# Loading half of a weight matrix ahead of the input and moving the tables behind it, at the start of a fused FFT-attention and feed-forward kernel

## The chip, the cores and the metric

The kernel runs on one core of a Trainium2 chip. The metric is the device time of one execution in microseconds (us); where several runs are given it is their median, with the range in brackets. The span of a profile is the time from its first to its last instruction and lies some 1.8 to 1.95 us below the device time of the same run. In the profiles PE is the matrix engine (TensorE) and PEld its loading of weights, DVE is VectorE, ACT is ScalarE, POOL is GpSimd, and SP is SyncE, which here issues DMAs. A profile is one execution.

## The reference, cut to what matters

```python
X  = rfft(x, axis=1)                        # x: 8 batches x 3008 x 256, f32
Yr = Xr @ w_r - Xi @ w_i + b_r              # w_r, w_i: 256 x 256
Yi = Xr @ w_i + Xi @ w_r + b_i
Yr, Yi = soft_threshold(Yr, 0.01), soft_threshold(Yi, 0.01)
y  = irfft(Yr + 1j * Yi, n=3008)            # viewed as 24064 rows of 256
r  = maximum(y @ w_in, 0)                   # w_in: 256 x 2048
out = (s * r * r + b) @ w_out               # w_out: 2048 x 256
```

## The kernel before: what the change and the argument touch

The Fourier transform over 3008 = 94 x 32 is done with matrices: `A_t` (94 points), `F_t` and `F_2` (32 points, forward), `T_t` (inverse). The first batch goes through alone, then the feed-forward part of one batch runs beside the transforms of the next. The first batch's x comes in eight half chunks on GpSimd's DMA queue, which casts f32 to f16. Everything else comes on SyncE's queue.

```python
A_t = cpool.tile(...); nc.sync.dma_start(out=A_t[0:N1, :], in_=A_d)
emit_load_x(0)                              # 8 half chunks, GpSimd's queue
for w in (w_r, w_i):                        # whole W, SyncE's queue: beside x
    st = rpool.tile([P, DC, D], F32, name="w_st", tag="rt")
    nc.sync.dma_start(out=st, in_=w.rearrange("(c p) e -> p c e", p=P))
    w_st.append(st)
...
def emit_load_inverse():                    # the whole tables
    nc.sync.dma_start(out=T_t[:, 0:H], in_=t_d[:, 0:H])
    nc.sync.dma_start(out=F_t[:, H:], in_=f_d)
    nc.sync.dma_start(out=F_2[1], in_=f_2_d)
    t_load = nc.sync.dma_start(out=T_t[:, H:], in_=t_d[:, H:])
    ...                                     # small things
def emit_load_weights():                    # w_in (2 loads), then w_out (4), GpSimd's queue
    ...
def place_w():                              # f32 staging -> f16 W_t, on ACT
    for i in range(2):
        nc.scalar.copy(out=W_t[:, :, i], in_=w_st[i])
def sum_w_out():                            # GpSimd: 7 adds, column sums of w_out for the bias b
    ...
# in the first batch, after each half chunk g (c, h = divmod(g, 2)):
if c == 2: emit_load_inverse(); place_f(slice(0, 4))     # only after its second half
if c == 1: place_w()
...
gate = nc.gpsimd.tensor_copy(out=w_in_t[0][0:1, 0:1], in_=F_t[0:1, H, 0:1])
with tc.issue_after(gate.ins):              # "the gate": waits until the rest of F_t is there
    emit_load_x(1)                          # second batch
    emit_load_weights()
...
# feed-forward, per 2 x 512 results: ACT takes the relu out of PSUM, DVE squares it
nc.scalar.activation(out=rt[:, :, 0:w], in_=ps[:, :, 0:w], func=AF.Relu)
nc.vector.tensor_tensor(out=gt[:, :, 0:w], in0=rt[:, :, 0:w], in1=rt[:, :, 0:w], op=ALU.mult)
```

The transform of a later batch writes `u` (three buffers), stores it to DRAM as `ud` and loads it back turned as `us`.

## Time and profile before

| | before |
|---|---|
| device time | 846.94 us (846.37 to 847.2, 3 runs) |
| span of the profile | 844.6 us |
| last half chunk of x reaches PE | 13.77 us |
| first matmul with W ("mixing starts") | 14.68 us |
| gate opens | 17.43 us |
| first output evacuated | 62.35 us |

The page's first rows give, for each engine, busy time, its share of the span and the number of instructions:

```profile
PE 835.1 (99%) x6654; PEld 601.3 (71%) x6654; DVE 694.7 (82%) x1034; ACT 640.6 (76%) x862; POOL 45.9 (5%) x73
```

Read this as: PE sets the time. Whatever the change wins or loses must show as PE starting its steady work sooner or later, or as PE idling, or else after PE's last matmul. Two moments are therefore followed: the start of mixing, and the first output. What lies between (47.67 us in this profile, 62.35 - 14.68) is called the middle; after the first output PE runs nearly without a gap.

### The profile page before, as it was taken

The numbers are of one execution on the slowest core, as the hardware profiler recorded it, in microseconds if no ns is written. First come the engines' busy times: TensorE is split into PE (matmuls) and PEld (weight loads), VectorE is DVE, ScalarE is ACT, GpSimd is POOL, SyncE is SP. The second block draws the span as 40 slices with busy tenths as digits, with TensorE's granted clock in tenths as the row PEclk, the third lists the DMA queues.
The fourth block names the chain that finished last, engine by engine and source line by source line (L and its number), as shares of the span: only waits on it lengthen the run. The fifth ranks groups of instructions, "written<-read, shape, count | busy, mean of one in ns | idle before, by whom it ended". The sixth has DMA issues, their size and how long they took to land.

```text
span 844.6 us, 17119 instructions
## 1 busy us (share of the span) xinstructions
PE 835.1 (99%) x6654; PEld 601.3 (71%) x6654; DVE 694.7 (82%) x1034; ACT 640.6 (76%) x862; POOL 45.9 (5%) x73
## 2 busy tenths in 40 slices
PE   8999999999999999999999999999999999999998
PEld 7857767777677766777677776777667777766765
DVE  5999987888888988888888888798978888776674
ACT  5987887778778877788777787778877778666673
POOL 4630000000000001000000000000000000000000
PEclk9999999999999999999999999999999999999999
DMA  7955467224851367324761247613354223411111
GB/s 200 181 151 118 119 161 199 74 77 98 202 156 54 103 171 188 93 70 107 189 174 50 81 101 196 172 43 90 106 152 125 59 78 97 113 33 38 38 44 50
DMA packets 105939, 96.06 MB, mean 114 GB/s; under 512 B 9607, under 2 KB 97675, under 8 KB 104515
## 3 DMA queue, kind: packets, MB, share of 16 engines
q1 hardware_dynamic: 99362, 80.55, 32.9%
q0 software_dynamic: 6496, 14.42, 10.6%
q8 instruction: 52, 0.85, 0.4%
q14 instruction: 29, 0.23, 0.1%
HBM read 53.52 MB, written 46.66 MB: 119 GB/s over the span
## 4 chain that ended last, share of the span: by engine, by line
PE 92%; ACT 3%; DVE 2%; DMA 1%; issue 1%; POOL 0%; DVEq 0%; ACTq 0%; POOLq 0%
PE psa L852 38%; PE psh L781 37%; PE psf L647 4%; PE psf L582 3%; PE psf L633 2%; PE psf L677 2%; PE psf L618 2%; PE psf L730 2%; ACT rt L788 1%; DMA x<-in_x_dram 1%; PE psm L425 1%; POOL x L213 0%; ACT yt L170 0%; DVE z L463 0%; PE psf L456 0%
## 5 line engine op out<-in xcount | busy, mean ns | idle before, releaser
L788 ACT ACTIVATE rt<-psh 128x1024 f32<-128x1024 f32 (+2 forms) x384 | 387.2, 1009 | 120.2 <-PE psh L781 118.8
L795 DVE TENSOR_TENSOR gt<-rt 128x1024 f16<-128x1024 f32 (+2 forms) x319 | 382.3, 1202 | 94.4 <-ACT rt L788 93.4
L852 PE MATMUL psa<-w_out_t,gt 128*128 128x256 f16 (+1 forms) x3024 | 454.4, 272 | 0.1
L852 PEld LDWEIGHTS <-gt 128*128 128x128 f16 (+1 forms) x3024 | 300.9, 101 | 186.6 <-issue 1.1
L781 PE MATMUL psh<-yt,w_in 128*128 128x512 f16 (+1 forms) x1344 | 396.8, 378 | 0.2 <-ACT rt L788 0.2
L781 PEld LDWEIGHTS <-w_in 128*128 128x128 f16 x1536 | 142.7, 98 | 26.2 <-issue 1.2
L862 DVE SCALAR_TENSOR_TENSOR ost<-psa,s_bc,bias_bc 128x512 f32<-128x512 f32 (+2 forms) x97 | 71.1, 733 | 9.6 <-PE psa L852 7.9
L792 ACT ACTIVATE gt<-rt 128x1024 f16<-128x1024 f32 (+2 forms) x65 | 68.2, 1050 | 0.9
L652 DVE TENSOR_TENSOR ring<-psf,s 128x512 f16<-128x512 f32 x84 | 57.6, 685 | 3.3 <-PE psf L647 3.2
L170 ACT CAST v<-psf 128x512 f16<-128x512 f32 x77 | 44.8, 582 | 19.4 <-PE psf L677 19.4
L170 ACT CAST xf<-psf 128x512 f16<-128x512 f32 x79 | 46.3, 586 | 8.8 <-PE psf L618 8.8
L781 PE MATMUL psh<-tail,w_in 128*128 128x512 f16 (+1 forms) x192 | 52.1, 353 | 0.0
L170 ACT CAST u<-psf 96x512 f16<-96x512 f32 x74 | 42.8, 580 | 11.2 <-PE psf L582 10.9
L647 PE MATMUL psf<-W_g,xf 128*128 128x256 f16 x336 | 50.4, 273 | 0.0
L170 ACT CAST yt<-psf 128x480 f16<-128x480 f32 (+2 forms) x76 | 39.0, 520 | 14.7 <-PE psf L730 14.2
L213 POOL DMA_DIRECT2D x<-in_x_dram x36 | 18.8, 527 | 432.9 <-PE psf L582 431.7
L582 PE MATMUL psf<-x,A_t 94*96 94x512 f16 x102 | 38.9, 382 | 1.0 <-ACT yt L170 0.6
L658 DVE TENSOR_TENSOR ring<-ring,high 128x512 f16<-128x512 f16 x84 | 35.6, 423 | 2.3
L659 DVE TENSOR_TENSOR ring<-ring 128x512 f16<-128x512 f16 x84 | 35.6, 423 | 2.1
L657 DVE TENSOR_TENSOR ring<-ring,low 128x512 f16<-128x512 f16 x84 | 35.5, 422 | 1.6
L647 PEld LDWEIGHTS <-xf 128*128 128x128 f16 x336 | 32.9, 98 | 4.1 <-issue 0.2
L730 PE MATMUL psf<-C_t,vs 96*128 96x96 f16 x448 | 33.2, 205 | 0.0
(100 smaller groups left out, 508.6 us busy)
## 6 DMA issues: line engine op xcount, KB each, us to landing
out_dram<-ost SPq DMA_DIRECT2D x152, 128.0 KB
ud<-u SPq DMA_DIRECT2D x28, 384.0 KB
us<-ud SPq DMA_DIRECT2D x28, 384.0 KB
vd<-v SPq DMA_DIRECT2D x42, 256.0 KB
vs<-vd SPq DMA_DIRECT2D x14, 768.0 KB
x<-in_x_dram POOLq DMA_DIRECT2D x28, 376.0 KB, 6.3
ring<-ring SPq DMA_DIRECT2D x280, 32.0 KB
out_dram<-ost SPq DMA_DIRECT2D x16, 120.0 KB
```

The costliest lines, as they stand in the source:

```text
L170: return None, nc.scalar.copy(out=dst, in_=src)
L582: nc.tensor.matmul(ps[0:96, :], A_t[0:N1, :], x16[(b, c)][0:N1, j * D : (j + 2) * D], start=True, stop=True,)
L647: nc.tensor.matmul(ps[:, r, :], xt[:, 2 - r, dc], W_g[:, dc, r], start=(dc == 0), stop=(dc == DC - 1),)
L652: nc.vector.tensor_tensor(out=t, in0=ps, in1=hold[i // 2][:, i % 2].unsqueeze(1).to_broadcast([P, 2, D]), op=ALU.add,)
L658: nc.vector.tensor_tensor(out=m, in0=m, in1=high, op=ALU.min)
L730: nc.tensor.matmul(ps[:, j * 96 : (j + 1) * 96], vs[(b, h)][:, k, ec * P : (ec + 1) * P], C_t, start=True, stop=True,)
L781: nc.tensor.matmul(o, w_in_t[dc][:, mc * P : (mc + 1) * P], r, start=(dc == 0), stop=(dc == DC - 1),)
L788: nc.scalar.activation(out=rt[:, :, 0:w], in_=ps[:, :, 0:w], func=AF.Relu)
L792: nc.scalar.activation(out=gt[:, :, 0:w], in_=rt[:, :, 0:w], func=AF.Square)
L795: nc.vector.tensor_tensor(out=gt[:, :, 0:w], in0=rt[:, :, 0:w], in1=rt[:, :, 0:w], op=ALU.mult)
L852: nc.tensor.matmul(ps[0:size, h, :], gts[(ti, mc // 2)][:, mc % 2, sub * size : (sub + 1) * size], w_out_t[:, mc, :], start=(mc == 0), sto ...
L862: nc.vector.scalar_tensor_tensor(out=ost[0:size, 0:k], in0=ps[0:size, 0:k], scalar=s_bc[0:size], in1=bias_bc[0:size].unsqueeze(1).to_broad ...
```

## The change

The intent is to let x, which bounds the first 14 us, arrive sooner. Only the columns e = 0..127 of W, those that the first mixing needs, are loaded beside x; the other half comes behind it. The small tables are placed one chunk earlier, so that ACT and DVE are free when x ends, and the loads of the whole tables start half a chunk later. The diff is whole:

```diff
--- before.py
+++ after.py
@@ -234,7 +234,9 @@
     w_st = []
     for w in (w_r, w_i):
         st = rpool.tile([P, DC, D], F32, name="w_st", tag="rt")
-        nc.sync.dma_start(out=st, in_=w.rearrange("(c p) e -> p c e", p=P))
+        nc.sync.dma_start(
+            out=st[:, :, 0:P], in_=w.rearrange("(c p) e -> p c e", p=P)[:, :, 0:P]
+        )
         w_st.append(st)
 
     b_g = cpool.tile([P, 2, D], F32, name="b_g")
@@ -274,6 +276,10 @@
 
     def emit_load_inverse():
         nc.sync.dma_start(out=T_t[:, 0:H], in_=t_d[:, 0:H])
+        for st, w in zip(w_st, (w_r, w_i)):
+            nc.sync.dma_start(
+                out=st[:, :, P:], in_=w.rearrange("(c p) e -> p c e", p=P)[:, :, P:]
+            )
         nc.sync.dma_start(out=F_t[:, H:], in_=f_d)
         nc.sync.dma_start(out=F_2[1], in_=f_2_d)
         t_load = nc.sync.dma_start(out=T_t[:, H:], in_=t_d[:, H:])
@@ -320,9 +326,11 @@
     def blocks(t):
         return t.rearrange("p q (r a k) -> p q r a k", r=2, a=2)
 
-    def place_w():
+    def place_w(ec):
+        e = slice(ec * P, ec * P + P)
         for i in range(2):
-            nc.scalar.copy(out=W_t[:, :, i], in_=w_st[i])
+            copy = nc.vector.tensor_copy if ec else nc.scalar.copy
+            copy(out=W_t[:, :, i, e], in_=w_st[i][:, :, e])
 
     def place_f(q):
 
@@ -385,22 +393,22 @@
                 last_act = on_act or last_act
             with tc.issue_after(last_pe.ins):
                 last_pe = keep_awake(5)
+            if g == 6:
+                with tc.issue_after(last_dve.ins):
+                    second = [st[:, :, P:] for st in w_st]
+                    for t in (T_t[:, 0:H], *second, F_t[:, H:], F_2[1], T_t[:, H:]):
+                        nc.vector.memset(t[0:1, 0, 0:1], 0.0)
+                emit_load_inverse()
             if h == 0:
                 continue
             if c == 0:
                 with tc.issue_after(last_dve.ins):
                     nc.vector.memset(F_c[0:1, 4, 0, 0:1], 0.0)
                 emit_load_forward()
-            if c == 2:
-                with tc.issue_after(last_dve.ins):
-                    for t in (T_t[:, 0:H], F_t[:, H:], F_2[1], T_t[:, H:]):
-                        nc.vector.memset(t[0:1, 0, 0:1], 0.0)
-                emit_load_inverse()
-                with tc.issue_after(last_dve.ins), tc.issue_after(last_act.ins):
+            if c == 1:
+                with tc.issue_after(last_act.ins), tc.issue_after(last_dve.ins):
                     place_f(slice(0, 4))
-            if c == 1:
-                with tc.issue_after(last_act.ins):
-                    place_w()
+                    place_w(0)
 
         gate = nc.gpsimd.tensor_copy(out=w_in_t[0][0:1, 0:1], in_=F_t[0:1, H, 0:1])
         with tc.issue_after(gate.ins):
@@ -533,6 +541,9 @@
             if i == 0:
                 with tc.issue_after(left[0].ins), tc.issue_after(left[1].ins):
                     place_f(slice(4, H))
+            if i == 3:
+                with tc.issue_after(left[0].ins):
+                    place_w(1)
             if 0 <= i - 1 < 2 * U:
                 fwd_dft(*steps[i - 1])
             if 0 <= i - 2 < 2 * U:
```

## The prediction

> **What bounds the kernel now.** I read the page first (how busy each engine is), then the busy time by stretch, then the chain that ended last in the first 22 us, then PE's timeline, the waits and the DMA queues there.
>
> The page says PE is busy 835.1 of 844.6 us, so nothing outside PE's 9.5 idle us can be won except by changing PE's work, and the change does not touch one matmul. The busy time by stretch (length, then PE, PEld, DVE, ACT, POOL busy with instruction counts, granted clock, DMA share, GB/s) shows where those 9.5 us lie:
>
> ```profile
> 0.00:5.50 5.50, 4.45 (x40) 4.18 (x40) 1.77 (x6) 1.28 (x1) 4.41 (x12) 1.00 0.57 138
> 5.50:14.68 9.18, 7.27 (x104) 6.53 (x105) 4.81 (x18) 5.17 (x11) 1.97 (x3) 0.81 0.95 182
> 14.68:45.56 30.88, 29.73 (x364) 24.98 (x365) 27.98 (x51) 27.76 (x53) 19.30 (x24) 1.00 0.93 201
> 45.56:844.60 799.04, 793.63 (x6148) 565.65 (x6146) 660.11 (x961) 606.38 (x798) 20.18 (x35) 1.00 0.41 109
> ```
>
> The change sits in the second row: from the first x (5.5 us) to the first matmul with W (14.68 us). There the DMA engines are 95% busy and no compute engine is above 80%, so I take this stage to be bound by the arrival of x. The chain of waits of the first 22 us confirms it (start, length, what):
>
> ```profile
> 1.22 3.71 POOL x L213 x7
> 4.92 8.80 DMA x<-in_x_dram
> 13.72 0.05 issue
> 13.77 0.36 PE psm L374 x4
> 14.12 0.02 issue
> 14.14 0.49 ACT ut L170
> 14.63 0.05 issue
> 14.68 1.28 PE psm L425 x10
> ```
>
> So the end of the stage is: eighth half chunk of x lands, PE transforms it at 13.77, ACT evacuates it at 14.14, mixing starts at 14.68. From landing to mixing is fixed work of 0.91 us. How much room lies before 13.77 is in PE's timeline (start, duration, what, idle before and its releaser):
>
> ```profile
> 12.70 0.34 PE L374 MATMUL psm<-A_t,x 94*128 94x96 f16 x4
> 12.87 0.33 PE L374 MATMUL psf<-A_t,x 94*128 94x96 f16 x4
> 13.04 0.44 PE L226 MATMUL psa<-ones 128*128 128x128 f16 x5
> 13.77 0.34 PE L374 MATMUL psm<-A_t,x 94*128 94x96 f16 x4 [0.28 <-DMA x<-in_x_dram]
> ```
>
> The five keep-awake matmuls start 0.055 us apart, so PE could take the last half chunk at about 13.04 + 5 x 0.055 = 13.32 us. It waits 0.45 us more (0.28 when the tails of the matmuls count as busy). **0.45 us is therefore the most that an earlier x can give**, unless the half chunks before it move too.
>
> DVE is the side branch. Its timeline holds what the change takes away from the end of x:
>
> ```profile
> 13.16 0.22 DVE L332 COPY F_t<-F_c 64x256 f16<-64x256 f16 x1
> ...
> 13.71 0.19 DVE L336 COPY F<-F_c 64x128 f16<-64x128 f16 x1
> 13.93 1.02 DVE L174 CAST ut<-psf 128x384 f16<-128x384 f32 x2
> ```
>
> The placing of four pairs delays the evacuation of the seventh half chunk to 13.93 and that of the eighth to 14.41, which ends at 14.96. This looks costly, but in the order of the built program the first four matmuls with W read only the half of `ut` that ACT wrote; the fifth is the first to wait for DVE, and it starts at 15.13. DVE is early by 0.17 us. Relieving DVE alone gives nothing.
>
> **What the Trainium skill says.** "DMA: Bandwidth & Descriptors", section "Queues, rings and completion order": each DMA engine goes round between the queues that have work, a packet at a time. So the W loads (SyncE's queue) take DMA time from x (GpSimd's queue), whoever issued first. The trace agrees. The DMA view of 3.3 to 6 us has both queues in it (share of 16 engines):
>
> ```profile
> q0 software_dynamic: 182, 0.33, 74.3%
> q1 hardware_dynamic: 372, 0.35, 37.8%
> ```
>
> and from 6 to 7.2 us, when W is in, x alone shows 139 packets in 1.2 us against 182 in 2.7 us here. The same page, "Why small descriptors are slow": each packet carries a fixed overhead. The trace agrees: packets of 1024 B took 50 ns (mean of 516), those of 512 B took 38 ns (128), those of 256 B about 29 ns. Halving the rows of W from 1024 to 512 B thus saves a quarter of the packet's time, not half.
>
> "TensorE: Matmul & The Clock Gate", part 1, has the clock at half rate in free-running windows of about 3.4 us, whose phase differs from run to run. The trace shows one such window, from 8.9 to 12.3 us (granted clock 0.81 in the stage), in which a half chunk takes PE 1.17 us against about 0.62. It is over before the last half chunk, so it costs the chain nothing here; in a run where it lies differently it may. That is part of my range.
>
> **The change part by part.**
>
> 1. *W in halves before x.* Before: 512 packets of 1024 B; now 512 packets of 512 B (the other 512 come after x). Saving: 512 x (50 - 38) ns = 6.1 us of DMA-engine time, over 16 engines 0.38 us. The engines are nearly full from 2.3 us, where W starts, until x's last packet lands at 13.35 us: by the trace's packet records x took 134.3 us of engine time, or 8.4 us of each of the 16, W 1.6 (512 x 50 ns / 16), the small tables 1.3, together 11.3 us in a stretch of 11.05 (packets overlap a little). So work taken out comes out of the end almost fully. Only W's packets before x starts (at 3.3 us, some 190 of 512) run in engines that are not quite full (39% in the view from 1.5 to 3.3 us), where the saving is partly lost. I take 0.3 us.
>
> 2. *Tables placed one chunk sooner.* On ACT, after the fourth half chunk (free at 10.54): F_t copy 0.40 plus two W halves. A W half is 256 columns; the whole W of 512 took 0.62 and the F_t copy of 256 took 0.40, so 0.40 each, some 0.33 apart. ACT is free at about 11.6; before, it was free from W at 11.5. The fifth evacuation shifts by 0.1 us, the sixth waits for PE anyway. On DVE the five small copies (0.74 us) run after the evacuation that ends at 10.94, until about 11.6, just when the next one is due (11.55). No one waits. At the end of x both engines are now empty. Worth on the chain: 0, as shown above, because ACT's evacuation follows PE within 0.03 us already.
>
> 3. *Whole tables half a chunk later, W's second half among them.* The first issue went out at 13.22; it now follows DVE's evacuation of the seventh half chunk, some 13.65, and six memsets, so about 13.7. In before x's last packet had landed at 13.35 and the first packet of these tables came at 14.19, so they did not collide with x; moving them gains nothing. It costs lateness: 0.5 us from the issue, two more issues of 0.47 us on SyncE, and 512 x 38 ns / 16 = 1.2 us of transfer. First half of T_t: before landed at 15.73, now 16.2, needed at 19.31. W's second half: about 17.3, copied on DVE from about 20.45. F_2: before 18.25, now about 20, needed at 21.63. Second half of T_t: before 20.22, now about 22, needed near 24.0. Every one still makes it, F_2 with the least room, 1 to 1.5 us.
>
> 4. *The second copy of W on DVE*, two instructions of 128x256, by DVE's copy of F_t some 0.25 us each. They stand after the second thresholding, in a gap of DVE of 1.01 us that ends with ACT (21.46). Hidden.
>
> 5. *The gate of the next loads.* F_t's landing releases GpSimd at 17.43; now about 18.7, and the loads of the second batch and of the two big weights move by 1.2 us. The second batch landed near 31 and is used at 38.8; GpSimd's sum of w_out ends at 46.1 and is used at 52.1. Hidden.
>
> Sum: 0.3 us off the start of mixing; nothing else on the chain. The chain after it (ACT and DVE in turn to 45 us, then PE) is carried over unchanged, so the end moves by the same 0.3: 846.94 - 0.3 = 846.6 us.
>
> **The rivals.**
>
> *A: nothing arrives sooner.* If 512 B packets beside x cost as much as 1024 B ones, or if the time is lost in the not-quite-full engines before 3.3 us, the last half chunk lands at 13.35 again. For it: W is done at 5.8 us, long before x ends. Against it: the engines' time adds up to the whole stretch. It gives 846.9.
>
> *B: the tables come too late.* If F_2 or F_t lands 2 us later than I reckon, PE stops at the fourth group of pairs (21.6 us) for up to 1 us. For it: the queue of SyncE already ran at only 260 to 390 GB/s there, and the loads of x and weights now start beside it. Against it: 1 us or more of room. It gives 847.2 to 847.9.
>
> *C: all of the wait goes.* If the half of W saved were worth its bytes (256 KB at some 200 GB/s is 1.3 us), x would land before 13.32 and PE would be the limit: 0.45 us, and a little more if the half-rate window moves away. 846.3 to 846.5.
>
> **Range and chances.** The three runs of before span 0.83 us, more than the effect. A clock window placed otherwise is worth up to about 1 us either way. So 845.8 to 847.4. Two per cent is 17 us; the whole stage that the change touches is 9 us long. Same: 0.98.
>
> **What would show it.** Right: the last half chunk reaches PE at 13.4 to 13.5 us with a shorter wait, mixing starts at 14.3 to 14.45, no wait on F_2, T_t or W_t anywhere, GpSimd's gate near 18.7 us, DVE copies of W in the gap before 21.5. Wrong: mixing at 14.68 or later (step 1), a wait of PE's weight load on a table between 20 and 25 us (step 3), DVE's thresholding pushed by the W copies (step 4), or a half-rate clock after 14 us.

## The result, and the profile after

The changed kernel took 847.3 us (846.47 to 849.27, 6 runs), the kernel before 847.07 us (846.37 to 848.92, 6 runs) in the same rounds. The ratio is 1.0004 with a 95% interval of 0.9989 to 1.0018. Ratios here are the mean time of one kernel's fast runs over that of the other's of the same rounds, so they are not quite the ratios of the medians quoted. The forecast of 0.3 us less did not come: if anything the median went up by 0.23 us.

The first rows of the page hardly differ; DVE has four instructions more (two copies of W, two memsets):

```profile
PE 834.3 (99%) x6654; PEld 599.8 (71%) x6654; DVE 695.2 (82%) x1038; ACT 640.0 (76%) x862; POOL 45.8 (5%) x73
```

Busy time by stretch, with the columns as in the prediction, cut at the same times:

```profile
5.50:14.68 9.18, 6.48 (x106) 5.10 (x106) 5.15 (x20) 4.83 (x11) 1.97 (x3) 1.00 0.84 157
14.68:45.56 30.88, 29.73 (x364) 24.92 (x363) 28.31 (x54) 27.91 (x53) 17.56 (x23) 1.00 1.02 213
```

In the stretch in which x arrives, the DMA share fell from 0.95 to 0.84 and the rate from 182 to 157 GB/s. Little of that is W itself, which was nearly all in by 5.5 us in both. It is mostly x, of which 130 KB more came before 5.5 us, and the tables' packets, which began at 14.57 instead of 14.19. The granted clock is 1.00 and no longer 0.81, yet the stretch barely shortened, which says again that PE's clock did not bound it. The chain of waits and PE's timeline show what x gained:

```profile
4.90 8.65 DMA x<-in_x_dram
...
13.60 0.36 PE psm L382 x4
...
14.51 1.28 PE psm L433 x10
```

```profile
12.82 0.45 PE L226 MATMUL psa<-ones 128*128 128x128 f16 x5
13.60 0.34 PE L382 MATMUL psm<-A_t,x 94*128 94x96 f16 x4 [0.34 <-DMA x<-in_x_dram]
```

The last half chunk came at 13.60 instead of 13.77, mixing started at 14.51 instead of 14.68, and the 0.91 us between them is unchanged. By the trace's packet records nearly all of x was there 0.38 us sooner (95% of its packets by 11.84 us, 12.22 before), but its last packet only 0.11 us sooner (13.24, 13.35 before). The gain was made at the front: x was issued at the same time (1.21 us, 1.22 before), yet its first packet came at 2.82 us instead of 3.34.

DVE's timeline has the two copies of W in the gap that the prediction named; thresholding still waits for ACT after them:

```profile
20.20 0.49 DVE L333 CAST W_t<-w_st 128x256 f16<-128x256 f32 x2
21.29 0.69 DVE L471 SCALAR_TENSOR_TENSOR z<-psf,m 128x512 f16<-128x512 f32 x1 [0.61 <-ACT m L469]
```

Of the 0.17 us, 0.14 were still there at 544 us. Then PE waited for a part of `us` that comes back from DRAM, which it did not do in the profile before:

```profile
544.57 0.40 PE L629 MATMUL psf<-F_t,us 128*128 128x128 f16 x4 [1.15 <-DMA us<-ud]
```

SyncE waited 4.5 us for the store of `ud` there, against 2.9 us before. That made up 1.3 of the 1.5 us by which this profile is longer than the one before. But it is one event in one profile.

Another 0.36 us were lost after the last output, and no run was made for it. At the program's end SyncE goes through nine waits, each for two semaphores, in a fixed order and some 0.06 us apart when nothing holds them up (the views leave such instructions out; the trace has them). Before, the semaphore of the last store (116) stands in the ninth wait; in the changed kernel the two loads more have moved that store to another one (110), which stands in the third, so that six waits follow after the store has landed. From its landing to the end of the span it takes 0.93 us before and 1.29 us after. Over all 20 profiles it is 0.91 to 0.93 us in the eight with W whole and 1.28 to 1.30 us in the twelve with the two loads more, w_halves_only among them: the steadiest difference of all. Device time seems to see less of it, since the changed kernel's runs lie 1.80 us above their spans in the mean and those of the kernel before 1.95; why is open.

The other thing that moved is GpSimd. Its timeline before and after, cut to the gate and to the sum of w_out (start, duration, what, idle before and releaser):

```profile
17.43 0.18 POOL L405 COPY w_in<-F_t 1x1 f16<-1x1 f16 x1 [8.24 <-DMA F_t<-fwd_rest]
...
37.41 1.15 POOL L344 TENSOR_TENSOR acc<-w_out_t 128x512 f32<-128x512 f16 x1 [1.57 <-DMA w_out_t<-in_moe_w_out_dram]
...
44.91 1.16 POOL L344 TENSOR_TENSOR w_sum<-acc,w_out_t 128x512 f16<-128x512 f32 x1
```

```profile
20.10 0.18 POOL L413 COPY w_in<-F_t 1x1 f16<-1x1 f16 x1 [11.87 <-DMA F_t<-fwd_rest]
...
39.08 1.15 POOL L352 TENSOR_TENSOR acc<-w_out_t 128x512 f32<-128x512 f16 x1 [3.43 <-DMA w_out_t<-in_moe_w_out_dram]
...
46.69 1.16 POOL L352 TENSOR_TENSOR w_sum<-acc,w_out_t 128x512 f16<-128x512 f32 x1
```

The gate opened 2.67 us later, not 1.2 to 1.3 as predicted, and the sum ended at 47.85 us instead of 46.07. DVE's first four squarings began right then:

```profile
47.81 4.67 DVE L795 TENSOR_TENSOR gt<-rt 128x1024 f16<-128x1024 f32 x4 [1.43 <-ACT rt L788]
```

```profile
47.63 4.70 DVE L806 TENSOR_TENSOR gt<-rt 128x1024 f16<-128x1024 f32 x4 [1.41 <-ACT rt L799]
```

In this profile the sum was out of the way just in time: 4.70 us against 4.67. A repeat had less luck.

### The profile page after: what moved, and what is told of

Same layout as the page of the kernel before. It is cut to its first block, busy times and chain, and to the rows that moved or that the text cites. A ratio compares the mean times of both kernels' runs of the same rounds, so it can differ in the third digit from the quotient of the medians.

```text
span 846.1 us, 17129 instructions
## 1 busy us (share of the span) xinstructions
PE 834.3 (99%) x6654; PEld 599.8 (71%) x6654; DVE 695.2 (82%) x1038; ACT 640.0 (76%) x862; POOL 45.8 (5%) x73
## 4 chain that ended last, share of the span: by engine, by line
PE 91%; ACT 3%; DMA 3%; DVE 2%; issue 1%; POOL 0%; DVEq 0%; ACTq 0%; SPq 0%; POOLq 0%
PE psh L792 37%; PE psa L863 37%; PE psf L658 4%; PE psf L593 3%; PE psf L644 2%; PE psf L629 2%; PE psf L688 2%; PE psf L741 2%; ACT rt L799 1%; DMA x<-in_x_dram 1%; DMA ud<-u 1%; PE psm L433 1%; DMA us<-ud 0%; POOL x L213 0%; ACT yt L170 0%
## 5 line engine op out<-in xcount | busy, mean ns | idle before, releaser
L792 PE MATMUL psh<-tail,w_in 128*128 128x512 f16 (+1 forms) x192 | 52.1, 353 | 0.0
L213 POOL DMA_DIRECT2D x<-in_x_dram x36 | 18.7, 525 | 433.0 <-PE psf L593 431.8
L629 PE MATMUL psf<-F_t,us 128*128 128x128 f16 x336 | 32.6, 219 | 1.3 <-DMA us<-ud 1.1
```

Source lines behind the costliest of these rows:

```text
L629: nc.tensor.matmul(ps[:, :, dc, j, :], t[:, q, dc * P : (dc + 1) * P], F_t[:, 2 * i + j, :], start=True, stop=True,)
L792: nc.tensor.matmul(o, w_in_t[dc][:, mc * P : (mc + 1) * P], r, start=(dc == 0), stop=(dc == DC - 1),)
```

## The experiments

Four theories were carried into the runs. *Chance*: the wait at 544 us is the scatter of a trip through DRAM and does not come back. *Slot*: the two loads added move later loads to other DMA semaphores, so that `us` waits in every run of the changed kernel. *x gained little*: the half of W saves less at the end of x than reckoned. *Gate*: the late gate makes the sum of w_out, or the stores of `u`, collide with the start of the feed-forward part. Eighteen kernels or repeats ran, in five calls; those of a call ran on one chip beside 11 runs of the kernel before. What follows rests on moments and durations inside the profiles.

### Repeats: before_again, after_again, after_third

No edit; the two kernels as they are.

> The kernel before, unchanged: how much of the difference is chance. Theory (the change moves only the landing of x's last half chunk; waits of the middle of the kernel for the trip through DRAM, us<-ud, come and go by chance): mixing (first matmul with W) starts within 0.15 us of 14.68, the time lies within 846.3 to 849 as before, and this execution too may show a wait of PE for us<-ud somewhere, of 0 to 2 us in all. Rival (that wait of 1.1 us at 544 us belongs to the changed kernel alone): no such wait here, and five times that spread less than 0.9 us.

> The changed kernel, unchanged. Theory: mixing starts at 14.3 to 14.6; the wait of 1.1 us for us<-ud at 544 us is gone or sits elsewhere; ratio of the times 0.9995 to 1.0005. Rival (two more DMAs on SyncE shift every later semaphore slot by two, and that makes the wait): the wait for us<-ud is at 544 us again, 1 us or more, and the time is 0.5 to 1.5 us over before.

> The changed kernel a third time. If its late gate eats the gain: gate at 19.5 to 21, in the profile either a wait for the DMA of u near 46 us or squarings over 4.67 us in two cases of three, and a median 0.2 to 0.8 us over that of order_again. If it is chance: median within 0.2 us of order_again's.

Measured: before_again 846.99 us (846.44 to 849.14), ratio to the other runs of the same kernel 0.9999 [0.9983, 1.0014]; after_again 847.45 us (846.39 to 848.77), 1.0001 [0.9987, 1.0016]; after_third 847.12 us (846.16 to 849.65), 0.9998 [0.9979, 1.0016].

The wait at 544 us was absent from after_again and 0.24 us in after_third. A kernel whose order of loads is fixed would show it each time, so the slot theory falls for this wait, and chance stands. (The loads added do move later DMAs to other semaphores; the cost of that stands at the program's end, as said above.) (The forecast on whole times: after_third was to lie 0.2 to 0.8 us over order_again if the late gate costs, and its median did, by 0.44 us, with intervals far wider.) In after_again the gate opened at 20.63, and GpSimd and DVE did this:

```profile
41.34 1.15 POOL L352 TENSOR_TENSOR acc<-w_out_t 128x512 f32<-128x512 f16 x1 [4.69 <-DMA w_out_t<-in_moe_w_out_dram]
...
48.98 2.02 POOL L352 TENSOR_TENSOR w_sum<-acc,w_out_t 128x512 f16<-128x512 f32 x1
```

```profile
48.21 6.14 DVE L806 TENSOR_TENSOR gt<-rt 128x1024 f16<-128x1024 f32 x4 [1.31 <-ACT rt L799]
```

The sum's last add took 2.02 us, not 1.16, and four squarings took 6.14 us, not 4.67. Taken singly, the squarings show what happened:

```profile
48.21 1.77 DVE L806 TENSOR_TENSOR gt<-rt 128x1024 f16<-128x1024 f32 x1 [1.31 <-ACT rt L799]
49.91 2.18 DVE L806 TENSOR_TENSOR gt<-rt 128x1024 f16<-128x1024 f32 x1
```

The two engines took turns. The sixth add ended at 48.90 us and the first squaring 1.08 us later, at 49.98; the last add ended 1.02 us after that, at 51.00, and the second squaring again 1.08 us after it, at 52.08. The third and fourth squarings took their usual 1.21 us. The same 1.08 to 1.09 us lie between the end of an add and the end of the squaring that overlaps it in every profile in which they meet. ACT also waited for a buffer of `u`, that is for the store that empties it; in the view of waits from 44 to 56 us:

```profile
ACT u L170 <- DMA ud<-u: 1.2, 1, 1.2
```

The middle took 49.82 us instead of 47.67. The kernel before is not free of this: in before_again the gate opened at 18.70, the sum ended at 48.60, the squarings took 5.31 us and the middle 48.31.

### Parts alone: w_halves_only, place_only, late_only

Each applies one part of the change to the kernel before. w_halves_only loads W in halves and copies the second on DVE, with the table loads where they were:

```diff
-        nc.sync.dma_start(out=st, in_=w.rearrange("(c p) e -> p c e", p=P))
+        nc.sync.dma_start(
+            out=st[:, :, 0:P], in_=w.rearrange("(c p) e -> p c e", p=P)[:, :, 0:P]
+        )
 ... second halves after T_t[:, 0:H], place_w(0) at c == 1, place_w(1) at i == 3
```

> Before with W in halves alone; its second half behind the first half of T_t, issued where before issues the whole tables; the four pairs placed where before places them. Theory: this part alone holds the gain, mixing at 14.3 to 14.6, x's last packet 0.1 to 0.4 us sooner than 13.35. Rival (it is the placing of the pairs, off DVE and ACT at the end of x, that gave the 0.17 us): mixing at 14.6 to 14.8. It has the two more DMAs too, so the rival of the semaphore slots expects the wait for us<-ud here as well.

Measured: 847.21 us (846.51 to 847.81), ratio 0.9998 [0.9983, 1.0013]; mixing at 14.28, gate 18.98, sum ends 45.78, squarings 4.67, middle 47.66. Mixing came sooner and nothing was lost in the middle.

place_only moves the placing of four pairs to c == 1:

```diff
             if c == 1:
-                with tc.issue_after(last_act.ins):
+                with tc.issue_after(last_act.ins), tc.issue_after(last_dve.ins):
+                    place_f(slice(0, 4))
                     place_w()
```

> Before with the tables of four pairs placed one chunk of x sooner, nothing else. Theory: no gain, mixing within 0.1 us of before's in the same call, since DVE had 0.17 us to spare. Rival of the placing: mixing 0.15 us or more sooner. No further DMA, so the rival of the semaphore slots expects no wait for us<-ud.

Measured: 847.86 us (846.7 to 849.29), ratio 1.0006 [0.9989, 1.0022]; mixing 14.85, gate 17.82, sum ends 47.15, squarings 4.67, middle 47.48. Mixing lay 0.21 us from before_again's, a little outside the 0.1 stated. Five of its six runs had a listed clock of 0.998 or less (see "Sorting by the clock" below). No gain at the start of mixing, as expected of a part that only relieves engines that wait for x.

late_only moves the loads of the whole tables from c == 2 to g == 6:

```diff
+            if g == 6:
+                with tc.issue_after(last_dve.ins):
+                    for t in (T_t[:, 0:H], F_t[:, H:], F_2[1], T_t[:, H:]):
+                        nc.vector.memset(t[0:1, 0, 0:1], 0.0)
+                emit_load_inverse()
```

> Before with the whole tables' loads half a chunk of x later, nothing else. Theory: no gain at mixing (within 0.1 us of before), the gate 0.4 to 0.9 us later than before (18.0 to 19.3), the sum of w_out later by as much; squarings 4.67 to 5.3 us. Rival (later loads leave x alone and mixing comes sooner): mixing 0.15 us or more sooner than 14.64.

Measured: 846.91 us (846.55 to 849.19), ratio 1.0 [0.9986, 1.0013]; mixing 15.04, gate 18.56, sum ends 47.41, squarings 4.67, middle 47.67. Mixing came later than the 0.1 us stated, as the scatter of the starts allows (see "Why the prediction was wrong"). The later issue alone costs the gate about a microsecond and leaves the sum just inside.

### The dose: gate_late, gate_far, gate_far_no_sum, no_sum

These change when the gate opens, or take the sum away. gate_late is the kernel before with a gate that waits for the last table:

```diff
-        gate = nc.gpsimd.tensor_copy(out=w_in_t[0][0:1, 0:1], in_=F_t[0:1, H, 0:1])
+        gate = nc.gpsimd.tensor_copy(out=w_in_t[0][0:1, 0:1], in_=T_t[0:1, H, 0:1])
```

> Before with one suspected cost enlarged: GpSimd's gate for the loads of the second batch and of the big weights reads the last table (second half of T_t) in place of F_t, so that it opens near 20.8 us instead of 17.4 to 18.7; W, pairs and tables as before. New theory (the change costs where I had called the gate hidden: the later loads push GpSimd's sum of w_out past 47.7 us, where DVE starts to square, and the two slow each other): the sum ends at 48.5 to 51, DVE's first four squarings take 5.3 to 6.2 us instead of 4.67, the end comes 0.5 to 1.5 us later than the start of mixing accounts for. Rival (the 5.3 and 6.1 us seen are chance, the gate does not matter): 4.67 us and nothing later.

Measured: 847.28 us (846.69 to 848.23), ratio 1.0001 [0.9988, 1.0015]; gate 20.75, sum ends 47.29, squarings 4.67, middle 48.04. The sum was expected to end between 48.5 and 51 and did not: the weights came faster after this gate than after the changed kernel's. So this dose missed its target, and its 0.37 us in the middle are not the sum's; ACT waited 0.9 us for the store of `u`.

gate_far, on the kernel before, opens the gate later still:

```diff
+            if i == 4:
+                gate = nc.gpsimd.tensor_copy(out=w_in_t[0][0:1, 0:1], in_=vt[0:1, 0, 0, 32:33])
+                with tc.issue_after(gate.ins):
+                    emit_load_x(1)
+                    emit_load_weights()
```

> Before with GpSimd's gate behind an evacuation of DVE near 23.4 us, 3 us later than in the changed kernel; nothing else. If a later gate costs (GpSimd's sum of w_out beside DVE's first squarings, and the stores of u beside the late loads): the sum ends at 50 us or later, DVE's first four squarings take 5.5 us or more, and mixing to first output takes 1 us or more longer than the 47.67 us of the undisturbed executions; time 1 to 3 us over before. If it does not: 47.67 us again and the time of before.

Measured: 848.61 us (848.32 to 850.43), ratio 1.0021 [1.0, 1.0041]; gate 23.79, sum ends 50.97, squarings 5.88, middle 49.13. This is the only kernel whose runs all lie above the usual: the fastest of six took 848.32 us, while 9 of the 11 runs of the kernel before beside it took 847.14 us or less. A late gate alone can cost about 2 us of device time, though the interval of the ratio just reaches 1.

gate_far_no_sum adds one more edit. It gives a wrong result, since the bias then lacks most of the sum:

```diff
-        for q in range(2, MC, 2):
+        for q in (MC - 2,):
             nc.gpsimd.tensor_tensor(
-                out=w_sum if q == MC - 2 else acc, in0=acc if q > 2 else w_out_t[:, 0:2],
+                out=w_sum if q == MC - 2 else acc, in0=w_out_t[:, 0:2],
```

> The same with six of the seven additions of the sum left out (wrong result on purpose). It parts the two costs of a late gate. If GpSimd's sum is the one: squarings 4.67 us, mixing to first output 47.7 us. If the stores of u are delayed by the loads: ACT waits for the DMA of u near 46 us by 0.9 us or more here too, and some 0.4 to 0.9 us of the loss stays.

Measured: 848.26 us (846.62 to 850.69), ratio 1.0013 [0.9992, 1.0034]; squarings back at 4.67, middle 48.25. The squarings' loss is gone with the sum, and 0.58 us of the middle's loss remain, with this wait beside it:

```profile
ACT u L170 <- DMA ud<-u: 1.1, 1, 1.1
```

So a late gate goes with two costs. The sum beside the squarings is shown, since taking it away takes the loss away. The late stores of `u` are argued: what the middle loses beyond the squarings grows with ACT's wait for them (0.25, 0.37, 0.58 and 0.68 us for waits of 0.7, 0.9, 1.1 and 1.2 us in gate_far, gate_late, gate_far_no_sum and after_again), but no run removed that wait alone.

no_sum is the changed kernel with the same edit (a wrong result, too):

> The changed kernel with six of the seven additions of GpSimd's sum of w_out left out (wrong result on purpose). New theory: with the sum gone from 47 to 51 us, DVE's first four squarings take 4.67 us although the gate is as late as in the changed kernel (near 20.3), and the lead of 0.2 to 0.3 us at mixing is whole at 62 us unless ACT waits for the DMA of u. Rival (DVE is slowed by the late DMA traffic, not by GpSimd's sum): 5 us or more again.

Measured: 846.53 us (846.46 to 847.59, 5 runs), ratio 0.9994 [0.9981, 1.0006]; gate 19.67, squarings 4.67, middle 47.66. With the sum gone, the changed kernel loses nothing in the middle, though its gate is late. The lead at mixing was expected whole at the first output, and was (62.15 us, 62.35 in the first profile before).

### Repairs: ft_first, ft_and_w_out_first, order_again, order_only, f_c_late

ft_first is the changed kernel with F_t, which the gate waits for, loaded first:

```diff
     def emit_load_inverse():
+        nc.sync.dma_start(out=F_t[:, H:], in_=f_d)
         nc.sync.dma_start(out=T_t[:, 0:H], in_=t_d[:, 0:H])
...
-        nc.sync.dma_start(out=F_t[:, H:], in_=f_d)
```

> The changed kernel with F_t loaded first of the tables, ahead of T_t and the second half of W, so that the gate opens near 16.8 us instead of 20.1 to 20.6. New theory: the sum of w_out ends by 47 us, the squarings take 4.67 us, the lead of mixing (0.15 to 0.3 us) is still there at the end, apart from waits of us<-ud. Rival (nothing of it matters, the middle of the kernel scatters by itself): no order between this and the changed kernel in the time of the first square or in the sum's end.

Measured: 847.23 us (846.41 to 849.35), ratio 1.0001 [0.9987, 1.0015]; gate 17.35, sum ends 46.87, squarings 4.67, middle 47.66. The gate is back where the kernel before had it.

ft_and_w_out_first and order_again are one kernel, which also loads w_out, whose sum takes 8.5 us, ahead of w_in:

```diff
     def emit_load_weights():
-        for dc in range(DC):
-            nc.gpsimd.dma_start(out=w_in_t[dc], in_=moe_w_in[dc * P : (dc + 1) * P, :])
         for q in (slice(q, q + 4) for q in range(0, MC, 4)):
...
+        for dc in range(DC):
+            nc.gpsimd.dma_start(out=w_in_t[dc], in_=moe_w_in[dc * P : (dc + 1) * P, :])
```

> The changed kernel with F_t first among the tables and w_out loaded before w_in, so that GpSimd's sum starts as soon as GpSimd is free at 35.8 us and ends near 44 us. If the two costs of the late gate are what ate the gain: squarings 4.67 us, mixing to first output 47.7 us in the profile, mixing at 14.1 to 14.5, and the median of the times 0.2 to 0.6 us under before. If the scatter has nothing to do with the gate: median as the changed kernel's, 847.2 to 847.5.

> The changed kernel with F_t first and w_out before w_in, again. If the late gate eats the gain: mixing at 14.1 to 14.5, mixing to first output 47.65 to 47.7 us, median 846.3 to 846.8, at or under before. If it is chance: median anywhere between 846.5 and 847.5.

Measured: 846.7 us (846.33 to 847.4), ratio 0.9993 [0.9975, 1.0011], and 846.68 us (846.01 to 846.98, 5 runs), ratio 0.9987 [0.9972, 1.0003]; gate 17.51 and 17.16, sum ends 43.91 and 43.47, middle 47.65 and 47.68. Of what was stated, order_again's whole time came, while its mixing (13.79) lay before the 14.1 to 14.5; ft_and_w_out_first was to have a median 0.2 to 0.6 us under before's and had one 0.14 us over it (846.56), which its interval does not tell from either. The squarings of order_again, from DVE's timeline:

```profile
46.93 4.67 DVE L806 TENSOR_TENSOR gt<-rt 128x1024 f16<-128x1024 f32 x4 [1.43 <-ACT rt L799]
```

order_only applies both edits to the kernel before, with W whole:

> Before with F_t first and w_out before w_in; W whole, pairs and tables where before has them. If W in halves is worth 0.3 us by itself: mixing at 14.5 to 15.0, mixing to first output 47.65 to 47.7 us, median 0.2 to 0.5 us over order_again's, if the scatter lets it be seen. If W in halves is worth nothing: mixing at 14.1 to 14.5.

Measured: 846.9 us (846.4 to 847.22, 5 runs), ratio 0.9991 [0.9976, 1.0006]; mixing 14.80, gate 18.38, sum ends 44.45, middle 47.67.

f_c_late, on the changed kernel, takes the remaining F_c away from x as well and loads it with the whole tables:

```diff
     def emit_load_forward():
         load_f_c(slice(4, H))
-        nc.sync.dma_start(out=sel_t, in_=S_d)
...
+                emit_load_forward()
                 emit_load_inverse()
             if c == 0:
...
-                emit_load_forward()
+                nc.sync.dma_start(out=sel_t, in_=S_d)
```

> The changed kernel with the second part of F_c (128 KB, which came beside the last packets of x) behind x as well. If the last half chunk waits for the slowest DMA engines and these are held up by F_c: x's last half chunk reaches PE at 12.9 to 13.3 instead of 13.5, mixing at 13.8 to 14.2, unless F_c is then late for the placing near 15.9. If the tail is x's own: 13.4 to 13.6 again.

Measured: 846.89 us (846.27 to 848.42), ratio 0.9998 [0.9979, 1.0017]; mixing 13.76, squarings 5.27, middle 48.85. Mixing began 0.7 us sooner than in the changed kernel, but order_again, without this edit, began at 13.79, so one profile does not tell the edit from scatter. Then 0.58 us were lost before the first feed-forward matmul (31.46 us after mixing, 30.88 in the changed kernel). Up to the third thresholding nothing was lost (6.77 and 6.78 us after mixing); then PE waited for the rest of F_2:

```profile
21.39 0.23 PE L463 MATMUL psf<-g,F 128*128 128x128 f16 x1 [0.46 <-DMA F<-fwd_rest_i]
```

It was issued at 15.42 us (15.53 in the changed kernel), but behind F_c's 128 KB as well, and mixing had begun 0.75 us sooner. This is rival B of the prediction, in a kernel that squeezes the tables further.

### Sorting by the clock: changed_five, reordered_five, w_out_first_five

After 15 runs the medians, those of place_only and of the two gate_far kernels aside, lay within 1 us of each other, with intervals of the ratios some 2 to 4 us wide. The scatter itself has a pattern. Sorted by the mean granted clock listed with each run, the kernel before has a mean span of 844.8 us at 0.999 or more, and at 0.998, 0.997 and 0.995 its means are 845.79, 846.04 and 846.76 (14, 7 and 5 runs, the last call's included). Keeping only runs at 0.999 or more gave 844.81 us for before (26 runs), 845.39 for the changed kernel (15) and 844.57 for the reordered one (9). A sort found after the fact proves little, so it was tested on three more kernels, with its numbers stated first. changed_five is the changed kernel, reordered_five the kernel of order_again, and w_out_first_five the changed kernel with w_out ahead of w_in but F_t where it was, so that the gate stays late.

> The changed kernel once more, judged by the spans of those runs alone whose granted clock is 0.999 or more, against runs of the kernel before of the same call by the same rule. The theory (0.50 us won at the start of mixing, about 1 us lost between mixing and first output because the gate opens late) expects the changed kernel 0.2 to 0.9 us longer. The rival (the loads' lateness is hidden, as the prediction had it, and the difference seen so far is scatter) expects it 0 to 0.5 us shorter.

> The changed kernel with F_t loaded first and w_out ahead of w_in, judged in the same way at a clock of 0.999 or more. The theory expects it 0.5 to 1.1 us shorter than the changed kernel of this call and 0 to 0.5 us shorter than the kernel before; first four squarings 4.67 us, gate 17 to 18 us. The rival of scatter expects the three kernels within 0.3 us of each other.

> The changed kernel with only w_out loaded ahead of w_in; the gate stays late (19.4 to 20.7 us). If the loss is all GpSimd's sum running beside the squarings, the sum now ends before 47.3 us, the squarings take 4.67 us, and mixing to first output is 47.6 to 47.8 us. If the late stores of u count as well, ACT or DVE still wait 0.5 us or more for a buffer of u near 46 us, and mixing to first output is 48.0 to 48.4 us though the squarings take 4.67 us. Span at a clock of 0.999 or more: at or below the kernel before in the first case, 0.1 to 0.5 us above the reordered kernel in the second.

Measured over all runs: changed_five 847.64 us (846.08 to 848.17, 5 runs), ratio 1.0007 [0.9995, 1.0019]; reordered_five 847.03 us (846.37 to 848.77, 5 runs), 1.0006 [0.9994, 1.0018]; w_out_first_five 847.22 us (845.74 to 850.44, 6 runs), 1.0014 [0.9997, 1.0031]; before 846.67 us (846.46 to 849.6, 11 runs). At a clock of 0.999 or more, mean spans:

| | before | changed | reordered | w_out first |
|---|---|---|---|---|
| this call (runs) | 844.86 (9) | 845.45 (4) | 844.80 (3) | 844.3 (2) |
| all calls (runs) | 844.82 (35) | 845.41 (19) | 844.62 (12) | 844.3 (2) |

The changed kernel came out 0.59 us longer than before in the new call, inside the 0.2 to 0.9 stated and outside what the rival of hidden loads allowed (four runs against nine; as large a difference comes up in 8% of random relabellings of these 13); the reordered kernel 0.65 us shorter than the changed one, also inside. Spans leave out what device time adds: by device time the same runs give 0.40 us in the new call, and over all calls 0.42. Four runs that span 844.3 to 846.1 are thin by themselves; with all 19 against 35, as large a difference came up 4 times in 20,000 random relabellings. But 15 of these 19 are the runs on which the sort was found, and they come from several calls. Without the sort the changed kernel's mean span is 0.34 us longer (23 runs against 61), which comes up in 21% of relabellings. The reordered kernel's 0.20 us below the kernel before came up in 14% of them and is not shown. Its gate was 18.51, above the 17 to 18 stated.

The profiles of the three: changed_five had its gate at 20.87, its sum end at 48.84, and

```profile
47.80 5.53 DVE L806 TENSOR_TENSOR gt<-rt 128x1024 f16<-128x1024 f32 x4 [1.41 <-ACT rt L799]
```

with a middle of 48.51. w_out_first_five parts the gate from the sum. Its gate was just as late, 21.04, but its sum was early:

```profile
43.65 1.15 POOL L352 TENSOR_TENSOR w_sum<-acc,w_out_t 128x512 f16<-128x512 f32 x1
```

```profile
48.30 4.67 DVE L806 TENSOR_TENSOR gt<-rt 128x1024 f16<-128x1024 f32 x4 [1.32 <-ACT rt L799]
```

Its middle took 47.80 us, and no wait for a store of `u` of 0.5 us or more stood there. That is the first of the two cases stated: with a late gate and an early sum, the squarings lose nothing. It is one profile, and the wait for `u` is absent from three of the changed kernel's four as well, so it does not say how often that wait comes. But of the 3.71 us that those four lost in the middle together, the squarings account for 3.06. In whole times nothing was gained: its ratio is 1.0014, and four of its six runs lie under 0.999, which the sort leaves out.

### All profiles beside each other

The four squarings take 4.67 us when alone. What they take more than that, and what the middle takes more than 47.67 us, go together where ACT does not wait for `u` and no table is late (us):

| profile | gate | sum ends | four squarings | more than 4.67 | middle more than 47.67 |
|---|---|---|---|---|---|
| before | 17.43 | 46.07 | 4.67 | 0 | 0 |
| before_again | 18.70 | 48.60 | 5.31 | 0.64 | 0.64 |
| after | 20.10 | 47.85 | 4.70 | 0.03 | 0.03 |
| after_third | 19.44 | 48.33 | 5.37 | 0.70 | 0.69 |
| changed_five | 20.87 | 48.84 | 5.53 | 0.86 | 0.84 |
| after_again | 20.63 | 51.00 | 6.14 | 1.47 | 2.15, and 1.2 of wait for `u` |
| gate_far | 23.79 | 50.97 | 5.88 | 1.21 | 1.46, and 0.7 of wait for `u` |
| gate_late | 20.75 | 47.29 | 4.67 | 0 | 0.37, and 0.9 of wait for `u` |
| gate_far_no_sum | 23.40 | (one add) | 4.67 | 0 | 0.58, and 1.1 of wait for `u` |
| f_c_late | 20.27 | 48.26 | 5.27 | 0.60 | 1.18, and 0.46 of wait for F_2 |
| no_sum | 19.67 | (one add) | 4.67 | 0 | -0.01 |
| w_out_first_five | 21.04 | 44.80 | 4.67 | 0 | 0.13 |
| ft_first | 17.35 | 46.87 | 4.67 | 0 | -0.01 |
| order_again | 17.16 | 43.47 | 4.67 | 0 | 0.01 |
| reordered_five | 18.51 | 44.59 | 4.67 | 0 | -0.01 |

The five profiles left out (w_halves_only, place_only, late_only, ft_and_w_out_first, order_only) have 4.67 us and a middle of 47.48 to 47.67. Where the sum ends before the squarings begin, 46.9 to 48.4 us, they take 4.67 us; where it ends later, they stretch, and the middle with them, one for one but for the waits named.

The gate is not all that sets the end of the sum. In the 13 profiles with w_in loaded first and the whole sum, 26.5 to 30.4 us lie between the two: w_halves_only opened its gate at 18.98 and ended its sum at 45.78, before_again opened at 18.70 and ended at 48.60. What makes that difference was not followed.

## Why the prediction was wrong

**Step 1 (W in halves) was right, and nearly right in size.** The first profile shows 0.17 us, but one profile says little: mixing starts scatter from 14.47 to 15.06 us with W whole and from 13.79 to 15.04 with W in halves. The eight profiles with W whole have a mean start of 14.78 us; the eleven with W in halves and F_c beside x, one of them with a half-rate clock from 11.4 us to the end of x, have 14.44. That is 0.34 us, with a standard error of some 0.13 worked out from the scatter within the two groups. The four profiles of the changed kernel alone have 14.51, 14.40, 14.32 and 14.68, mean 14.48, or 0.30 us.

That the size came out so well is in part luck, for two errors offset each other. W's packets of 512 B took about 29 ns, not the 38 taken over from F_c, so the saving by the prediction's own formula is 512 x (50 - 29) / 16 = 0.67 us, not 0.38. And the prediction thought that what is saved before x starts is partly lost, and that the rest comes out of the end almost fully. In fact the gain enters at the front and is partly lost towards the end: x's first packet came at 2.69 to 2.90 us in all twelve profiles with W in halves and at 3.12 to 3.43 in all eight with W whole; on average (without f_c_late) the first packet came 0.54 us sooner, 95% of x 0.50, and the last packet 0.32. Why x starts sooner is not settled; w_halves_only (2.70) shows that W in halves alone does it. Rival A (nothing) lies 2.6 standard errors from the mean of 0.34 us; rival C (all 0.45 us) lies less than one from it and is not excluded.

**Step 2 (tables sooner) and step 4 (copies of W on DVE) were right.** place_only brought no earlier mixing, and the copies lie in the gap before 21.5 us. **Step 3 (late tables) was right** in that no weight load of PE waited on F_2, T_t or W_t between 20 and 25 us in the changed kernel's four profiles; rival B did not come there. Of the variants, w_out_first_five (0.2 us) and f_c_late (0.69 us) had such a wait on F_2. In the first changed profile the last packet of F_2 came at 19.70, and that of T_t's second half at 21.70.

**Step 5 ("The gate of the next loads", ending in "Hidden") failed, twice.** First in size: it put the gate at "about 18.7", that is, it took only the 1.2 us of transfer. Its own step 3 had named 0.5 us of later issue and two more issues of 0.47 us on SyncE besides, all of which stand ahead of F_t: 0.5 + 0.94 + 1.2 = 2.6, and 17.43 + 2.6 = 20.0. The changed kernel's four profiles have 20.10, 20.63, 19.44 and 20.87. The terms were there, and were not added. In the first profile they can be read off: F_t was issued at 15.02 us instead of 13.64, of which 0.39 is the later start and 0.99 the two issues ahead of it, and the gate opened 1.29 us later still. The 17.43 is one profile, though; before_again has 18.70, and the means of the two kernels are 2.2 us apart. Second in kind: "Hidden" was concluded from the one reader of the sum that had been looked at, its use at 52.1 us. But a computation can cost while nobody waits for its result. The sum's adds and the squarings disturb each other when they run at the same time, and the squarings begin at 47.5 us. With its sum ending at 46.07, the kernel before had 1.7 us to spare in its first profile, of which nothing was said. With the 1.2 us predicted, the sum would have ended at 47.3, still just clear; with 2.67 it was not (47.85, squarings at 47.63).

The Trainium skill would have told it: "SBUF — State Buffer", section "Who interferes with whom", says that a DVE instruction with two inputs in SBUF contends with a GpSimd instruction that reads SBUF. The squaring has both inputs in SBUF, and so has the add. The trace agrees: 1.16 us becomes 2.02 for an add, 4.67 becomes up to 6.14 for four squarings, and the instructions that meet end one after the other.

**The carry-over ("The chain after it [...] is carried over unchanged, so the end moves by the same 0.3") failed as well, and in every profile.** The two loads that step 1 adds were reckoned as issues on SyncE; nobody asked what they do to the program's end. There they put the last store on an earlier place in SyncE's closing waits, and from its landing to the end of the span it takes 1.28 to 1.30 us instead of 0.91 to 0.93. This alone takes back as much of the span as step 1 won.

**The sum of the steps.** Won at the start of mixing: 0.30 us. Lost in the middle by the four profiles of the changed kernel: 0.03, 0.69, 0.84 and 2.15, mean 0.93; by the two profiles of the kernel before: 0 and 0.64, mean 0.32. Lost at the end: 0.36. So the net of the span is 0.93 - 0.32 + 0.36 - 0.30, about 0.7 us more; with four and two profiles, the scatter within them makes the standard error of the loss in the middle about 0.5 us. The spans say 0.58 us more at equal clock and 0.34 over all runs, the device times 0.42 and 0.19. The forecast gain is there at the start of mixing, and it is gone again at the end; that the changed kernel is slower as a whole is likely by the sort, but not shown.

**What stays open.** The size of the loss in runs without a profile is only inferred from spans at equal clock. Why the store of `u` comes late in some late-gate profiles (after_again, gate_far_no_sum, gate_late) and not in others (changed_five, w_out_first_five) is not settled. The trip of `us` through DRAM cost PE 1.15 us in one of the 20 profiles and 0 to 0.3 in the others, which no run tied to the change. Nor is it settled whether a kernel influences its own clock: 19 of 23 runs of the changed kernel reached 0.999, 35 of 61 of the kernel before, and sorting by the clock assumes that it does not. Nor was it tried to keep the last store on its old semaphore. The reordered kernel has the better profile in the middle, though the end costs it the same 0.36 us, and is faster than the changed kernel at equal clock; that it beats the kernel before is not shown (all runs: 0.9993, 0.9987 and 1.0006, each with an interval that holds 1).

## What to carry to other kernels

When a change makes a side branch later, look not only at who waits for its result but at what it will now run beside; two engines that share a path to memory cost each other time with no wait in the profile, only as longer instructions, so compare the duration of the same instruction, one by one, in both kernels. Add up every term of a delay that the working has already named, before calling it hidden. Follow a gain to the last instruction: compare the time after the last output too, since one DMA more or less can change it. With effects of a few tenths of a microsecond, collect an intermediate moment over many profiles, and sort whole runs by granted clock, with the rule stated before the runs that test it.

## What the Trainium skill lacked or had wrong

- "SBUF — State Buffer", "Who interferes with whom", gives the rule but no measured cost for this pair. Here a squaring of 128x1024 f32 on DVE, 1.21 us when alone, ended 1.08 us after the GpSimd add of 128x512 that it overlapped and took up to 2.18 us, and an add went from 1.16 to 2.02 us. Neither instruction shows a wait; only the durations tell.
- "DMA: Bandwidth & Descriptors", "Why small descriptors are slow": no duration for a packet of a queue that runs beside a casting stream of another. Here the 1024 B packets of W took 50 to 60 ns in the mean of a profile, and 512 B took 38 ns for F_c and about 29 for W.
- The same page gives no figure for how the end of a load lags its bulk. x's last packet came 1.4 us after 95% of its packets (13.24 against 11.84 us), and taking 0.38 us from the bulk took 0.11 us from the end.
- None of the pages cited has what a program's closing waits cost. Here SyncE's nine waits stand 0.06 us apart, and it took 0.91 to 0.93 or 1.28 to 1.30 us from the last landing to the end of the span, by the place of the last store's semaphore among them.
- "TensorE: Matmul & The Clock Gate", part 1, was borne out in that the half-rate window is about 3.4 us long and lies elsewhere from run to run: 4 of the 20 profiles have one while x arrives, starting at 7.35, 7.75, 8.91 and 11.36 us, and in w_out_first_five it lay on the last half chunk (four matmuls 0.52 instead of 0.34 us; mixing at 15.04). None of the sections cited gives what clock scatter of a whole run is worth: here spans of one kernel rose by 1.0 us in the mean from 0.999 and more (844.82) to 0.998 (845.79).
